# Attention output of the last 64 queries by pairs of heads in the two column halves of the PE array, and their residual added by PE

## The chip, the cores and the metric

One Trainium2 chip, of which one core is used. The metric is the device time of one execution in microseconds (us), here the median of the runs shown. Beside the runs there is one profiled execution, whose trace all durations come from.

## What is computed

Block-wise causal attention on 8 batches with 8 heads, 576 positions and 64 values per head, followed by an MLP-mixer layer. The inputs are float32; the kernel computes in bfloat16 with float32 sums.

```python
scores = q @ k.T / sqrt(64)              # (8, 8, 576, 576)
scores = where(pos_i // 64 >= pos_j // 64, scores, -1e9)
attn   = softmax(scores)
x      = (attn @ v)                      # heads side by side: (8, 576, 512)
h = relu(x.T @ w_tok1) @ w_tok2          # over the 576 positions, 256 hidden
u = x + h.T
out = u + relu(u @ w_ch1) @ w_ch2        # over the 512 channels, 1536 hidden
```

576 is 4.5 times 128. So each batch has four full blocks of 128 query rows and a rest of 64 rows (positions 512 to 575), and the same holds for the keys.

## The kernel before

**How the order is made.** The kernel doesn't issue instructions as it runs through its loops. Every step is added to a planner (class `Plan`) with an engine, an assumed cost, its predecessors, a priority and the PSUM bank that it takes. `Plan.run` plays the steps through in assumed time, `Plan.search` repeats this a thousand times with shaken priorities and keeps the order with the earliest end. The instructions are then emitted in that order, one fixed sequence for each engine. A change of any cost or step therefore gives another order everywhere. A step also has a mode: 0 where the matmul uses the whole 128x128 PE array, 1 for the score matmuls, which use strips of 32 rows, and 2 for matmuls of 64 columns. The planner charges 0.1 us for a change of mode.

**Attention** (`attention`, and `first_attention` for batch 0). A batch's heads are handled as two groups of four (`hg` 0 and 1). For a group, `score_set` (L554) computes transposed scores, keys in the partitions and queries along the free side, with four heads at once in the four 32-row strips of the array; ACT takes the exponentials (L573) into the one buffer `e_sb[hg]`, and DVE clears the masked parts (L579). The keys 512 to 575 are seen only by the last 64 queries; their exponentials for all heads go to `et_sb`.

`head_out` then makes a head's output. The exponentials are the stationary operand (`lhsT`), 128 queries at a time, and the values with a column of ones are the moving operand of 65 columns, so that the last column of the sum is the softmax denominator. Query block I takes key blocks J = 0 to I: 1+2+3+4+5 = 15 matmuls (L602) into one PSUM bank. The fifth block (I = 4) has 64 queries only; the load takes 128 columns all the same, shifted by 64 in odd batches (`shift`), so that the 64 rows lie in partitions 0 to 63 in even and in 64 to 127 in odd batches. The other 64 columns are filler, for which `e_sb` has 64 more columns and `et_sb` is zeroed at the start. DVE takes the reciprocal of the five denominators (L624, 128x5) and multiplies (L630, 128x320) into `x_sb`, whose fifth block is row block 4.

**Token mixing.** `token_up` (L791) multiplies `x_sb` by `w_tok1`: for each half of the hidden side five accumulating matmuls of 512 columns, one for each row block; the fifth uses a copy of the weights with zeros in the half of the partitions that holds filler (`w1_sb[:, 4]` in even batches, `w1o_sb` in odd ones). RELU, then the down product (L884), to which DVE adds `x` (L899). The last 64 rows of two batches share one tile `um_sb` of 128 rows: four pairs. Their down product (L915) already works with the two halves of the PE's columns, one for each batch, and DVE adds the residual by two instructions of 64 partitions (L932).

**Channel mixing.** `channel_up` (L1002), `channel_up_mixed` (L1029), `channel_up_fast` (L1107), `channel_down` (L1322) and `channel_down_fast` (L1231) make the rest. The fast ones use a Strassen-like scheme. The change doesn't touch them.

**The start.** SP loads the keys and queries of batch 0, group 0. All other loads of the start are issued by POOL, one after another: keys and queries (L419), values (L468), weights (L487, L510, L519). Ahead of them POOL makes the identity and zeroes `et_sb` and the ends of `e_sb`; DVE fills the constant parts of `vals` and of `w1_sb` and `w1o_sb` (all at L343). PE runs matmuls on zeros[...] (L372, L379).

Of the kernel before, what the change touches and what calls it, by code (L numbers as in the profile page):

```python
# [22 lines left out]
class Op:  # L23
# [4 lines left out]
        "users", "need", "key", "waiting", "ready", "start", "end", "engine", "n", "mode", "at", "urgent", "until", "quick",  # L28
# [3 lines left out]
class Plan:  # L32
# [13 lines left out]
    def add(  # L46
        self, engines, cost, emit, deps=(), prio=0.0, take=(), give=(), xfer=None, mode=0, at=0.0,
        urgent=0, until=1e9, quick=False,
    ):

        o = Op()
        o.engines = (engines,) if isinstance(engines, str) else tuple(engines)
        o.cost = cost if isinstance(cost, dict) else {e: cost for e in o.engines}
        o.emit, o.prio, o.take, o.give, o.xfer = emit, prio, take, give, xfer
        o.mode, o.at, o.urgent, o.until, o.quick = mode, at, urgent, until, quick
        o.deps = list({id(d): d for d in deps if d is not None}.values())
        o.users, o.n = [], len(self.ops)
        self.ops.append(o)
        return o
# [39 lines left out]
    def run(self):  # L99
# [21 lines left out]
        while left:  # L121
# [13 lines left out]
            for e in ("PE", "ACT", "DVE", "POOL", "SP"):  # L135
                if busy[e] > t or e == "POOL" and landed[-8] > t:
                    continue
                for at, a in enumerate(avail[e]):
                    if self.fits(a[3]):
                        break  # L140
                else:
                    continue
                o = a[3]
# [52 lines left out]
def kernel(  # L196
# [40 lines left out]
    e_sb = ring(2, [128, 4, 1600], BF16, "e_sb")  # L237
# [86 lines left out]
    def reuse(key):  # L324
        return readers.pop(key, [])
# [13 lines left out]
    def init_tiles():  # L339
        def fill(engine, key, prio, *parts):  # L340
            for t, value in parts:
                def emit(o, t=t, value=value):
                    (nc.vector if engine == "DVE" else nc.gpsimd).memset(t, value)  # L343

                pads.setdefault(key, []).append(P.add(engine, 0.17 if engine == "DVE" else 0.5, emit, (), prio))

        for i, t in enumerate(kT):
            fill("DVE", ("kT", i), -1e4 + i, (t[:, S:640, :], 0.0))
        for i in range(2):
            fill(  # L350
                "DVE", ("v", i), -60 + 20 * i,
                (v1[i][64:128, 4, :, :], 0.0),
                (v1[i][:, 0:4, :, 64:65], 1.0),
                (v1[i][0:64, 4, :, 64:65], 1.0),
            )
            fill("POOL", ("e", i), -1e5 + 1, (e_sb[i][:, :, 1536:1600], 0.0))
            fill("POOL", ("et", i), -1e5, (et_sb[i], 0.0))
        fill("DVE", "zeros", -1e5, (zeros, 0.0))
        fill("DVE", "w1", -70, (w1_sb[64:128, 4, :], 0.0), (w1o_sb[0:64, :], 0.0))

        def emit(o):
            make_identity(nc, ident)

        pads["ident"] = [P.add("POOL", 0.6, emit, (), -1e6)]
# [119 lines left out]
    def load_token_weights():  # L484
        def load(dst, src, xfer, prio):
            def emit(o):
                nc.gpsimd.dma_start(out=dst, in_=src)  # L487

            return P.add("POOL", 0.66, emit, (), prio, xfer=xfer)

        done1 = [
            load(w1_sb[:, 0:4, :], moe_w_tok1[0:512, :].rearrange("(c p) t -> p c t", p=128), 32 * 0.06, 5.0),
            load(w1_sb[0:64, 4, :], moe_w_tok1[512:576, :], 4 * 0.06, 5.1),
        ]
        done2 = [
            load(w2_sb, moe_w_tok2.rearrange("(p c) s -> p c s", c=2), 8 * 0.25, 5.2)
        ]
        done1o = [load(w1o_sb[64:128, :], moe_w_tok1[512:576, :], 4 * 0.06, 12.0)]
        return (done1 + pads["w1"], done1 + done1o + pads["w1"]), done2
# [83 lines left out]
    def head_out(b, head, deps, prio, tail, urgent=0):  # L583
        hg, h = divmod(head, 4)

        ei = hg if b == 0 else b % 2
        vt, xt, et, e = v1[b % 2], x_sb[b % 3], et_sb[ei], e_sb[hg]
        ecol = ECOL_LAST if b == 0 and hg == 1 else ECOL
        shift = 0 if b % 2 == 0 else -64
        bank = {}  # L590

        def emit(o, chunks):
            u = bank_of(bank)[:, 0:330].rearrange("p (i c) -> p i c", c=66)
            for I in chunks:
                for J in range(I + 1):
                    if J < 4:
                        c = ecol[J] + 128 * (I - J) + (shift if I == 4 else 0)
                        w = e[:, h, c : c + 128]
                    else:
                        c = 64 + 128 * h + (64 * hg if b else 0) + shift  # L600
                        w = et[:, c : c + 128]
                    nc.tensor.matmul(  # L602
                        out=u[:, I, 0:65],
                        lhsT=w,
                        rhs=vt[:, J, head, 0:65],
                        start=(J == 0),
                        stop=(J == I),
                    )

        steps = ((0, 1, 3), (2, 4)) if b == 0 else (range(5),)  # L610
        av = None
        for chunks in steps:
            av = P.add(
                "PE", 0.0298 * (sum(chunks) + len(chunks)), lambda o, c=chunks: emit(o, c),
                [av, tail] + deps, prio, take=[(BANK, bank)] if av is None else (), urgent=urgent,
            )
        reads(("e", hg), av)
        reads(("et", ei), av)
        reads(("v", b % 2), av)
        ri = rinv[head % 4]  # L620

        def emit_rc(o):
            u = bank_of(bank)[:, 0:330].rearrange("p (i c) -> p i c", c=66)
            nc.vector.reciprocal(ri, u[:, :, 64:65])  # L624

        rc = P.add("DVE", 0.19, emit_rc, [av] + reuse(("rinv", head % 4)), prio - 1, urgent=urgent)

        def emit_mu(o):
            u = bank_of(bank)[:, 0:330].rearrange("p (i c) -> p i c", c=66)
            nc.vector.tensor_tensor(  # L630
                out=xt[:, :, 64 * head : 64 * head + 64],
                in0=u[:, :, 0:64],
                in1=ri.to_broadcast([128, 5, 64]),
                op=MULT,
            )

        mu = P.add("DVE", dve_cost(320), emit_mu, [rc], prio - 1, give=[bank], urgent=urgent)
        reads(("rinv", head % 4), mu)
        return mu

# [6 lines left out]
    def first_tail(hg, heads, deps, prio):  # L647
# [3 lines left out]
        def emit(o):  # L651
# [12 lines left out]
            "PE", 0.1, emit, deps + pads["kT", hg] + pads["et", hg], prio,  # L664
# [12 lines left out]
    def first_attention(ready, v_ready):  # L677
# [3 lines left out]
        for j in range(4):  # L681
# [36 lines left out]
            for h in heads:  # L718
                deps = exps + v_ready[hg] + pad + pads["e", hg]
                done.append(head_out(0, 4 * hg + h, deps, -2900 + j, tails[h], urgent=1))  # L720
        return done

    def attention(b, ready, v_ready):
        et = et_sb[b % 2]
        x_war = reuse(("x", b % 3))
        pad = pads["v", b % 2] + pads["et", b % 2]
# [6 lines left out]
        def tail():  # L733
            deps = ready[0] + ready[1] + pads["et", b % 2] + reuse(("et", b % 2))
# [10 lines left out]
        for hg in range(2):  # L745
# [19 lines left out]
            for h in range(4):  # L765
                deps = exps[h // 2] + v_ready[hg] + x_war + pad + pads["e", hg]
                done.append(head_out(b, 4 * hg + h, deps, prio + 1, tail_done[h // 2]))
# [14 lines left out]
    def token_up(b, cols, tts, xs, war, ready, prio, urgent=0):  # L782
        odd, xt, at = b % 2, x_sb[b % 3], aT[b % 2]
# [3 lines left out]
        def emit(o):  # L787
            for n, tt in enumerate(tts):
                for c in range(5):
                    wt = w1o_sb if c == 4 and odd else w1_sb[:, c]  # L790
                    nc.tensor.matmul(  # L791
                        out=bank_of(bank)[:, w * n : w * n + w],
                        lhsT=wt[:, tt : tt + 255 : 2],
                        rhs=xt[:, c, cols],
                        start=(c == 0),
                        stop=(c == 4),
                    )

        op = P.add("PE", mm_cost(w, 5 * len(tts)), emit, xs + ready[odd] + war, prio, take=[(BANK, bank)], urgent=urgent)
# [11 lines left out]
    def first_uT(x_done, a_done, w2_ready):  # L811
# [3 lines left out]
        for m in range(NDM):  # L815
            bank = {}

            def emit(o, m=m, bank=bank):
# [10 lines left out]
                "PE", mm_cost(128, 4), emit, x_done[2 * m : 2 * m + 2] + pads["ident"], -2700 + m,  # L829
# [27 lines left out]
    def token_mix(b, x_done, w1_ready, w2_ready):  # L857
# [10 lines left out]
        if b == 0:  # L868
            a_all = [
                token_up(0, slice(128 * m, 128 * m + 128), (0, 1), x_done[2 * m : 2 * m + 2], [], w1_ready, -2800 + m, 1)  # L870
# [37 lines left out]
        else:  # L908
# [3 lines left out]
            def emit(o, bank=bank):  # L912
                for t in range(NDT):
                    for i in range(2):
# [5 lines left out]
                            stop=(t == NDT - 1),  # L920
# [3 lines left out]
                "PE", mm_cost(512, 2) + 0.02, emit, a_even[pair] + a_all + w2_ready + um_free[pair], prio + 1.4,  # L924
                take=[(BANK, bank)], mode=2,
            )
            for i in range(2):
                reads(("a", i), op)
                r = slice(64 * i, 64 * i + 64)

                def emit(o, i=i, r=r, bank=bank):
                    nc.vector.tensor_tensor(  # L932
                        out=umt[r, :], in0=bank_of(bank)[r, :], in1=x_sb[(b - 1 + i) % 3][r, 4, :], op=ADD
                    )

                um_rows.append(P.add("DVE", dve_cost(512), emit, [op] + um_rows, prio, give=[bank] if i else ()))
                reads(("x", (b - 1 + i) % 3), um_rows[-1])

# [532 lines left out]
```

## Time and profile before

| | us |
|---|---|
| Median of 5 runs | 293.81 |
| All five | 293.16, 293.62, 293.81, 294.43, 299.16 |
| The profiled execution, its own time | 293.19 |
| Its span in the trace | 291.4 |
| Outside the span (293.19 - 291.4) | 1.8 |
| PE busy in the span | 284.6 |
| DVE busy in the span | 231.8 |
| ACT busy in the span | 170.1 |
| POOL busy in the span | 63.7 |
| Matmuls recorded in the trace | 3224 |

A row of the profile's groups gives the source line, the engine, the operation, what it writes and reads (buffer numbers left out), the array tile for PE, the shapes, how often it occurs, its busy time in us with the mean of one in ns, and the idle time of the engine ahead of it with what ended most of it. "PEld" are the weight loads of PE, which run beside its matmuls. [...]successive ones overlap, so their cost in a dense sequence is the distance of their starts. A few matmul records are missing from the trace. The granted clock of PE was 1.0 throughout.

### The profile page before, as it was taken

The page shows a single profiled execution, that of the slowest core. Times are in us where ns is not written, and L with a number is a line of the kernel's source. Part 1 is how long each engine was busy: PE and PEld are TensorE (multiplying, and loading weights), DVE is VectorE, ACT ScalarE, POOL GpSimd, SP SyncE. Part 2 cuts the span into 40 slices and gives each one's busy share as a digit, 9 for nine tenths or more (in the row PEclk, how much of TensorE's full clock was granted, in tenths as well). Part 3 has the DMA queues.
Part 4 walks back from the last instruction along what each step waited for, and adds up shares of the span by engine and source line. Part 5 has one row for each costly group of instructions (what it writes and reads, how often), then busy time and mean ns, then how long its engine had stood idle before and what let it go on. Part 6 is the DMA issues. An engine that isn't in the chain of part 4 may idle for free.

```text
span 291.4 us, 7678 instructions
## 1 busy us (share of the span) xinstructions
PE 284.6 (98%) x3224; PEld 179.3 (62%) x3244; DVE 231.8 (80%) x505; ACT 170.1 (58%) x241; POOL 63.7 (22%) x100
## 2 busy tenths in 40 slices
PE   8999999999999999999999999999999999999994
PEld 3566446456564766645776466884446888644883
DVE  5566669989687959897997877586989887798994
ACT  5897974758877663677564888432587303377000
POOL 9975545620800150430041000000000000000000
PEclk9999999999999999999999999999999999999999
DMA  8999999995996097991429003041001901230036
GB/s 209 157 201 207 210 186 184 231 188 136 126 172 90 2 128 176 166 177 38 74 20 209 3 2 72 2 164 36 3 0 33 167 2 72 97 122 0 1 100 227
DMA packets 64548, 31.99 MB, mean 110 GB/s; under 512 B 53121, under 2 KB 55297, under 8 KB 64513
## 3 DMA queue, kind: packets, MB, share of 16 engines
q0 software_dynamic: 44320, 17.34, 50.2%
q1 hardware_dynamic: 20192, 14.16, 18.6%
q8 instruction: 25, 0.41, 0.5%
q14 instruction: 11, 0.08, 0.1%
HBM read 35.85 MB, written 9.44 MB: 155 GB/s over the span
## 4 chain that ended last, share of the span: by engine, by line
PE 89%; DMA 5%; POOL 3%; issue 1%; DVE 0%; POOLq 0%
PE mm L1231 19%; PE mm L1002 15%; PE mm L602 9%; PE sc L554 9%; PE mm L1322 7%; PE mm L1107 6%; PE late L1107 6%; PE mm L791 5%; PE late L1231 4%; PE mm L884 4%; PE mm L1029 3%; DMA raws<-in_q_dram 3%; DMA w_sb<-in_moe_w_tok_dram 2%; POOL vals L468 2%; PE mm L915 1%
## 5 line engine op out<-in xcount | busy, mean ns | idle before, releaser
L573 ACT ACTIVATE e_sb<-sc 128x1024 bf16<-128x1024 f32 x95 | 92.4, 1026 | 34.3 <-PE sc L554 33.5
L468 POOL DMA_DIRECT2D vals<-in_v_dram x45 | 37.1, 843 | 41.1 <-PE sc L554 24.8
L1002 PE MATMUL mm<-uT,wc_sb 128*128 128x512 bf16 x192 | 46.1, 382 | 0.0
L439 DVE STREAM_TRANSPOSE turned<-raws 128x288 int32<-128x288 int32 (+1 forms) x65 | 40.4, 698 | 4.4 <-ACT raws L400 1.8
L554 PE MATMUL sc<-turned 32*128 32x64 bf16 (+4 forms) x744 | 35.4, 281 | 0.8 <-ACT e_sb L573 0.5
L602 PEld LDWEIGHTS <-e_sb 128*128 128x128 bf16 x896 | 31.0, 97 | 6.5 <-issue 3.6
L602 PE MATMUL mm<-vals,e_sb 128*128 128x65 bf16 x882 | 32.8, 193 | 0.1
L1002 PEld LDWEIGHTS <-wc_sb 128*128 128x128 bf16 x192 | 20.0, 115 | 20.3 <-issue 5.3
L630 DVE TENSOR_TENSOR x_sb<-mm,rinv 128x320 bf16<-128x320 f32 x63 | 29.7, 483 | 1.4
L1231 PEld LDWEIGHTS <-sums 128*128 128x128 bf16 x252 | 24.0, 98 | 4.9 <-issue 1.4
L1231 PEld LDWEIGHTS <-gT 128*128 128x128 bf16 x240 | 22.8, 98 | 5.0 <-issue 1.4
L777 ACT ACTIVATE gT<-mm 128x512 bf16<-128x512 f32 x36 | 21.6, 599 | 6.3 <-PE mm L1002 4.7
L554 PEld LDWEIGHTS <-turned 32*128 32x128 bf16 x752 | 12.6, 93 | 18.4 <-issue 14.8
L579 DVE MEMSET e_sb<- 64x128 uint32 (+1 forms) x72 | 10.5, 153 | 10.8 <-ACT e_sb L573 7.7
L1254 DVE TENSOR_TENSOR o_sb<-mm,u_sb 128x512 f32<-128x512 f32 x20 | 13.6, 685 | 6.4 <-PE mm L1231 6.3
L791 PE MATMUL mm<-x_sb,w_sb 128*128 128x512 bf16 (+1 forms) x97 | 17.8, 314 | 0.3
L779 DVE TENSOR_SCALAR gT<-mm 128x512 bf16<-128x512 f32 x15 | 10.3, 688 | 9.7 <-PE mm L1002 9.6
L1231 PE MATMUL mm<-wd_sb,sums 128*128 128x256 bf16 x132 | 16.1, 273 | 0.0
L899 DVE TENSOR_TENSOR u_sb<-mm,x_sb 128x512 bf16<-128x512 f32 x24 | 15.4, 681 | 0.8 <-PE mm L884 0.7
L1254 DVE TENSOR_TENSOR o_sb<-mm,o_sb 128x512 f32<-128x512 f32 (+1 forms) x19 | 12.1, 643 | 4.9 <-PE mm L1231 4.8
L1107 PEld LDWEIGHTS <-raws 128*128 128x128 bf16 x96 | 9.3, 98 | 10.4
L777 ACT ACTIVATE gmT<-mm 128x512 bf16<-128x512 f32 x9 | 5.4, 599 | 17.6 <-PE mm L1029 17.6
(145 smaller groups left out, 457.1 us busy)
## 6 DMA issues: line engine op xcount, KB each, us to landing
out_dram<-o_sb SPq DMA_DIRECT2D x14, 512.0 KB, 3.2
raws<-in_k_dram POOLq DMA_DIRECT2D x15, 288.0 KB, 6.7
raws<-in_q_dram POOLq DMA_DIRECT2D x15, 288.0 KB, 7.6
vals<-in_v_dram POOLq DMA_DIRECT2D x28, 128.0 KB, 6.1
wc_sb<-in_moe_w_ch_dram POOLq DMA_DIRECT2D x8, 192.0 KB, 7.1
wc_sb<-in_moe_w_ch_dram POOLq DMA_DIRECT2D x3, 512.0 KB, 10.3
out_dram<-o_sb SPq DMA_DIRECT2D x10, 128.0 KB, 2.4
vals<-in_v_dram POOLq DMA_DIRECT2D x15, 64.0 KB, 4.7
```

Of the source, the lines that this page charges most:

```text
L439: nc.vector.transpose(dst[:, 0:S, :] .rearrange("p s e -> p (s e)") .bitcast(I32) .rearrange("p (a k) -> p k a", k=NB)[:, k0:k1], raw2.bit ...
L468: nc.gpsimd.dma_start(out=dst, in_=src)
L554: nc.tensor.matmul(out=home(n)[:, c0 : c0 + w], lhsT=kT[i][r, j0 : j0 + 128, par], rhs=qT[i][r, i0 : i0 + w, par], start=(par == 0), stop= ...
L573: nc.scalar.activation(dst, sc[SC.index(note["pool"])][:, :, 0:n], EXP, scale=scale)
L602: nc.tensor.matmul(out=u[:, I, 0:65], lhsT=w, rhs=vt[:, J, head, 0:65], start=(J == 0), stop=(J == I),)
L630: nc.vector.tensor_tensor(out=xt[:, :, 64 * head : 64 * head + 64], in0=u[:, :, 0:64], in1=ri.to_broadcast([128, 5, 64]), op=MULT,)
L777: nc.scalar.activation(dst, src, RELU)
L791: nc.tensor.matmul(out=bank_of(bank)[:, w * n : w * n + w], lhsT=wt[:, tt : tt + 255 : 2], rhs=xt[:, c, cols], start=(c == 0), stop=(c == 4),)
L1002: nc.tensor.matmul(out=bank_of(bank), lhsT=wc1_sb[:, m, channels(cc)], rhs=uT[b % 2][:, :, m, :], start=(m == 0), stop=(m == NDM - 1),)
L1107: nc.tensor.matmul(out=bank_of(bank), lhsT=x(m), rhs=y[:, :, m, :], start=first and m == 0, stop=m == 1, skip_group_check=not first,)
L1231: nc.tensor.matmul(out=bank_of(bank)[:, 256 * i : 256 * i + 256], lhsT=x[:, kk, 128 * i : 128 * i + 128], rhs=y[:, kk], start=first and i ...
L1254: nc.vector.tensor_tensor(out=dst, in0=src, in1=other, op=ADD)
```

## The change

- `head_out` computes the four full query blocks only: 10 matmuls per head in place of 15; its reciprocal has 4 columns and its multiply 256.
- A new step `ends_out` makes the last 64 queries. Two heads run side by side: head 2p in array columns 0 to 63 (PSUM partitions 0 to 63), head 2p+1 in columns 64 to 127. A group of four heads is one step of 20 matmuls with loads of 64 columns, in mode 2; in batch 0 it is two steps of 10. A reciprocal (128x2) and a multiply (128x128) follow.
- So row block 4 of `x_sb` has another layout: even heads in partitions 0 to 63, odd heads in 64 to 127, 256 columns in use, in every batch. `token_up` handles it with two matmuls of 256 columns in place of one of 512: with the weights for the lower and for the upper partitions, each into its own 64-column pieces of the output. All batches now wait for both copies of the weights, so that the load of `w1o_sb` is asked for earlier (5.1 in place of 12.0).
- The residual of the paired last rows is added by PE: after the four matmuls of the down product, four more of 256 columns with halves of the identity as stationary operand. One copy, on DVE or ACT, replaces DVE's two adds.
- The planner gets a flag `stick`: such a step is taken only when the last PE step was in a tiled mode, and then ahead of all others; without it in the list PE goes on as before. All `ends_out` steps have it but those of batch 0 and the last one of all.
- Filler goes: `e_sb` has 1536 columns per head, `et_sb` and `e_sb` are not zeroed. The constant fills of `vals`, `w1_sb` and `w1o_sb` move from DVE to POOL, ahead of POOL's loads: 8 memsets in place of 4.

The planner orders everything anew, and the built orders of all engines differ from the start on.

```diff
@@ Plan.run
-                for at, a in enumerate(avail[e]):
+                at = None
+                tiled = e == "PE" and mode > 0
+                for n, a in enumerate(avail[e]):
+                    if a[3].stick > tiled or at is not None and not a[3].stick:
+                        continue
                     if self.fits(a[3]):
-                        break
-                else:
+                        at = n
+                        if a[3].stick or not tiled:
+                            break
+                if at is None:
                     continue
@@ init_tiles
-                pads.setdefault(key, []).append(P.add(engine, 0.17 if engine == "DVE" else 0.5, emit, (), prio))
+                pads.setdefault(key, []).append(P.add(engine, 0.17 if engine == "DVE" else 0.25, emit, (), prio))
...
-                "DVE", ("v", i), -60 + 20 * i,
+                "POOL", ("v", i), -1e5 + i,
...
-            fill("POOL", ("e", i), -1e5 + 1, (e_sb[i][:, :, 1536:1600], 0.0))
-            fill("POOL", ("et", i), -1e5, (et_sb[i], 0.0))
-        fill("DVE", "w1", -70, (w1_sb[64:128, 4, :], 0.0), (w1o_sb[0:64, :], 0.0))
+        fill("POOL", "w1", -1e5 + 2, (w1_sb[64:128, 4, :], 0.0), (w1o_sb[0:64, :], 0.0))
@@ load_token_weights
-        done1o = [load(w1o_sb[64:128, :], moe_w_tok1[512:576, :], 4 * 0.06, 12.0)]
-        return (done1 + pads["w1"], done1 + done1o + pads["w1"]), done2
+        done1o = [load(w1o_sb[64:128, :], moe_w_tok1[512:576, :], 4 * 0.06, 5.1)]
+        return done1 + done1o + pads["w1"], done2
@@ head_out
-        steps = ((0, 1, 3), (2, 4)) if b == 0 else (range(5),)
+        for chunks in ((0, 1), (2, 3)) if b == 0 else (range(4),):
...
-            nc.vector.reciprocal(ri, u[:, :, 64:65])
+            nc.vector.reciprocal(ri[:, 0:4], u[:, :, 64:65])
...
-                in1=ri.to_broadcast([128, 5, 64]),
+                in1=ri[:, 0:4].to_broadcast([128, 4, 64]),
@@ new
+    def ends_out(b, hg, pairs, deps, prio, urgent=0):
...
+        def emit(o):
+            for g, pair in enumerate(pairs):
+                for J in range(5):
+                    for i in range(2):
+                        h = 2 * pair + i
+                        if J < 4:
+                            c = ecol[J] + 128 * (4 - J)
+                            w = e[:, h, c : c + 64]
+                        else:
+                            c = 64 + 128 * h + (64 * hg if b else 0)
+                            w = et[:, c : c + 64]
+                        nc.tensor.matmul(
+                            out=bank_of(bank)[64 * i : 64 * i + 64, 66 * g : 66 * g + 65],
+                            lhsT=w,
+                            rhs=vt[:, J, 4 * hg + h, 0:65],
+                            start=(J == 0),
+                            stop=(J == 4),
+                        )
+
+        av = P.add(
+            "PE", 0.03 * 5 * n, emit, deps, prio, take=[(BANK, bank)], mode=2, urgent=urgent, stick=b > 0 and (b, hg) != (B - 1, 1),
+        )
...
+            nc.vector.reciprocal(ri, view(64, 65))
...
+            nc.vector.tensor_tensor(
+                out=xt[:, 4, c : c + 64 * n].rearrange("p (g d) -> p g d", d=64),
+                in0=view(0, 64),
+                in1=ri.to_broadcast([128, n, 64]),
+                op=MULT,
+            )
@@ token_up
-                for c in range(5):
-                    wt = w1o_sb if c == 4 and odd else w1_sb[:, c]
+                for c in range(4):
                     nc.tensor.matmul(
+                        out=ps, lhsT=w1_sb[:, c, tt : tt + 255 : 2], rhs=xt[:, c, cols], start=(c == 0), stop=False
+                    )
+                for i, wt in enumerate((w1_sb[:, 4], w1o_sb)):
+                    nc.tensor.matmul(
+                        out=ps.rearrange("p (g i d) -> p g i d", i=2, d=64)[:, :, i],
                         lhsT=wt[:, tt : tt + 255 : 2],
-                        rhs=xt[:, c, cols],
+                        rhs=xt[:, 4, cols.start // 2 : cols.stop // 2].rearrange("p (g d) -> p g d", d=64),
@@ token_mix
+                for n in range(2):
+                    for i in range(2):
+                        nc.tensor.matmul(
+                            out=bank_of(bank)[64 * i : 64 * i + 64, :].rearrange(
+                                "p (g n d) -> p g n d", n=2, d=64
+                            )[:, :, n],
+                            lhsT=ident[:, 64 * n : 64 * n + 64],
+                            rhs=x_sb[(b - 1 + i) % 3][:, 4, 0:256].rearrange("p (g d) -> p g d", d=64),
...
-                    nc.vector.tensor_tensor(
-                        out=umt[r, :], in0=bank_of(bank)[r, :], in1=x_sb[(b - 1 + i) % 3][r, 4, :], op=ADD
-                    )
...
+            def emit(o, bank=bank):
+                cast(o, umt, bank_of(bank))
+
+            um_rows.append(P.add(EVAC, evac_cost(512), emit, [op], prio, give=[bank]))
```

## The prediction

> **What bounds the kernel now.** I read the page's engine totals and the chain of work first.
>
> ```profile
> PE 284.6 (98%) x3224; PEld 179.3 (62%) x3244; DVE 231.8 (80%) x505; ACT 170.1 (58%) x241; POOL 63.7 (22%) x100
> ...
> PE   8999999999999999999999999999999999999994
> ...
> PE 89%; DMA 5%; POOL 3%; issue 1%; DVE 0%; POOLq 0%
> ```
>
> PE is busy in every slice and makes nine tenths of the chain. A busy PE need not be a dense PE, so next the chain in order of time (start, duration, what), and the timeline where the tile of the array changes.
>
> ```profile
> 49.19 0.90 PE mm L602 x30
> ```
> ```profile
> 60.34 1.03 PE L1322 MATMUL mm<-wc_sb,gT 128*128 128x512 bf16 x4
> 61.30 0.62 PE L915 MATMUL mm<-aT,w_sb 128*64 128x512 bf16 x4
> 61.85 0.63 PE L554 MATMUL sc<-turned 32*128 32x512 bf16 x8
> 62.42 0.35 PE L602 MATMUL mm<-vals,e_sb 128*128 128x65 bf16 x6
> ```
>
> Thirty matmuls of 65 columns take 0.90 us, 30 ns each. Four of 512 begin at 60.34 and should end their 4 x 0.216 us at 61.20; the next mode begins at 61.30, so the change costs 0.10 us. L915's four run as two concurrent pairs: 0.55 us to the next start, of which 2 x 0.216 are two steps and 0.12 the next change.
>
> I then added up the built order from the first L1002 to the last matmul (26.82 to 287.32 us in the trace, 260.5 us). Concurrent tiles counted once[...], its matmuls take 247.8 us; it has 103 changes of mode, after each of which the trace shows 0.10 us and another 0.01 to 0.03 us at the second step, 0.123 us in the mean, 12.7 us in all. The sum is 260.4 us: from 27 us on PE never waits for anyone. Its waits in the whole trace agree:
>
> ```profile
> PE mm L372 <- DVE wd_sb L343: 1.2, 1, 1.2
> PE sc L554 <- ACT e_sb L573: 0.5, 1, 0.5
> ```
>
> So a PE nanosecond saved after 27 us is a nanosecond of the end, and work of other engines there is free unless it makes PE wait. Before 27 us the bound is a chain over POOL, DMA, DVE and ACT.
>
> [...]
>
> ```profile
> L915 PEld LDWEIGHTS <-w_sb x16: 106/108/110, 61.3 to 205.1; 128*64 128x64 bf16 x16
> ```
> ```profile
> 61.30 0.14 PEld L915 LDWEIGHTS <-w_sb 128*64 128x64 bf16 x4 [0.42 <-issue]
> ```
>
> A load of 64 columns lasts 108 ns against 97 for L602's 128. But all four fit in 0.14 us, so the last starts 0.03 us after the first: the two tiles load together and a tile's second load follows some 28 ns after its first.
>
> **The change, part by part, after the first L1002** (14 of the 16 groups; batch 0 lies before).
> - L602 goes from 840 to 560 matmuls: 280 x 29.6 = -8.28 us.
> - `ends_out`: 280 matmuls as 140 concurrent steps. No row shows narrow matmuls in this mode. Below, a step can't beat its 65 columns, 29.6 ns. Above, if the two loads went one after another, it is [...]57 ns (estimate from the 28 ns between a tile's loads). The nearest row, 64 columns in four strips, has steps of 29 to 33 ns. I take 32: +4.48 us (4.14 to 8.0).
> - `token_up`: in 14 sums one matmul of 512 becomes two of 256, 218 against 216 ns: +0.04 us.
> - The residual: 16 matmuls, 8 concurrent steps of 256 columns at 109 ns: +0.87 us, in L915's mode, so without a change of its own.
> - Modes: the order has 116 changes in place of 103. Of the 13 places where `ends_out` now stands (one holds two groups) 11 follow a score set and lead back to the full array, so that one change becomes two. 13 x 0.115 us (the mean into steps of 65 columns is 0.112): +1.50 us. From below 13 x 0.10, from above 13 x 0.136.
> - DVE per group: 4 x (186 + 483) = 2.68 us becomes 4 x (186 + 417) + about 180 + 283 = 2.88 (417 is the row of a 256-column sum, 283 goes on in its line with 685 for 512): +2.8 us over 14 groups. The residual takes 2 x 0.685 from DVE and gives one copy to DVE or ACT: -2.7 us or more for four pairs. Nothing for the end: DVE stays near 80% and PE has other batches' channel products to run meanwhile. Without that cover it would be 0.2 us a group.
> - The banks and `e_sb`: one more short bank use per group. `e_sb[hg]` is held until the last 64 queries are done, and the next score set of that group, its exponentials and POOL's next loads of values queue behind. The old order ran without a stall at the same pressure; I put 0.1 us.
>
> Sum: -8.28 + 4.48 + 0.04 + 0.87 + 1.50 + 0.10 = -1.29 us.
>
> **The start.** L554 of batch 1 at 26.25 and L1002 behind it wait for two things at nearly the same time.
>
> ```profile
> 1.25 1.19 POOL L343 MEMSET vals<- 128x640 bf16 x2
> 2.39 0.56 POOL L343 MEMSET e_sb<- 128x256 bf16 x2
> 2.90 0.69 POOL L419 DMA_DIRECT2D raws<-in_k_dram  x1
> ```
> ```profile
> 22.91 0.49 DVE L630 TENSOR_TENSOR x_sb<-mm,rinv 128x320 bf16<-128x320 f32 x1
> ...
> 24.94 1.26 DVE L439 STREAM_TRANSPOSE turned<-raws 128x288 int32<-128x288 int32 x2 [0.38 <-DMA raws<-in_q_dram]
> ```
>
> First, the queries of batch 1 land at 24.92. POOL's memsets grow: 640 elements took 625 ns and 256 took 305, so 528, 32, 8 (twice) and 256 (twice) make 2.1 us, and most now wait for the one before (0.07 us, as the identity's second step did): 2.3 us against 1.65, and every load that POOL issues starts 0.65 us later. But the DMA engines are nine tenths busy from 2 us on, first with SP's loads until about 6 us, while POOL's first bytes move at 5.3; so most of it is absorbed in that backlog. `w1o_sb` now stands ahead of these queries: 32 KB at some 190 GB/s, 0.17 us. I take +0.3 us, bounds +0.1 and +0.85. Second, the last multiplies of batch 0, where DVE runs without a break: a pair of heads took 1.34 us, now 2 x (186 + 417) + 150 + 216 = 1.57 us; two pairs give +0.46 us ahead of the transposes. PE's saving there (0.3 us a group) is hidden behind ACT's exponentials, 1.03 us each. DVE's idle 0.38 us takes in part of both: together +0.4 us (0.1 to 1.2).
>
> Total -1.29 + 0.40 = -0.9 us: the profiled time goes from 293.19 to 292.3. The median shown lies 0.62 us above the profiled time; applied to it, 293.81 - 0.9 = **292.9 us**.
>
> **Rivals.**
> - *As forecast* (own range 292.2 to 293.6). Chance 0.46.
> - *Narrow steps at their floor and the start absorbed*: 140 x 29.6, changes at 0.10, start +0.1: -8.28 + 4.14 + 0.91 + 1.3 + 0.1 = -1.8 us, 292.0. For it: the fitted sum of before. Chance 0.11.
> - *The start takes it back*: +1.2 us in place of 0.4 gives -0.1 us, 293.7. For it: POOL heads the chain that ended last; against it, the saturated DMA. Chance 0.20.
> - *Slower by a new wait*: `stick` holds a group's last queries until a score set comes by, `token_up` needs all of `x`, and PE[...] stops. It decides from 0.9/14 = 0.065 us per group; at 0.15 us a group it is +2.1, in all +1.2 us, 295.0. Against it: the planner spread the work to no stall before. Chance 0.13.
> - *Slower, the pairs don't overlap*: the two column tiles load in turn, 57 ns a step, +3.5 us, in all +2.6, 296.4 us. Break-even at 38 ns. Against it: L915's loads 0.03 us apart. Chance 0.10. Here the change wouldn't do what it says.
>
> **Numbers.** About 0.3% (0.9 us) is what a measurement of this kernel can tell from no change. The forecast sits on that bound: of its 0.46 I count 0.33 as faster and 0.13 within; with the second case 0.44 faster; with the third 0.33 within; the two slower cases 0.23. The range, 291.8 to 295.0, reaches from the second case to the fourth and leaves out the fifth.
>
> **What would show it.** L655: twenty matmuls in 0.32 us, after a score set, with 0.1 us on each side (right), or 0.57 us (fifth case). L599 at 30 ns. PE's waits after 27 us: none of size, else the fourth case. The first L1075 at 27.2 us in place of 26.82; at 28 the third case. DVE near 232 us busy. I would be wrong if PE's dense stretch got longer than 259.2 us.

## The result and the profile after

| | before | after |
|---|---|---|
| Median | 293.78 us (79 runs) | 297.15 us (44 runs) |
| Lowest to highest | 293.02 to 299.97 us | 293.09 to 299.83 us |
| Profiled execution | 293.19 us, span 291.4 | 298.39 us, span 296.6 |
| Granted clock in it | 1.000 | 0.977 |
| First channel-up matmul (L1002, L1075) | 26.82 us | 33.19 us |
| From there to the last matmul | 260.50 us | 259.49 us |
| Ratio | | 1.0042, interval 1.0025 to 1.0059 |

The change made the kernel slower; the forecast was 292.9 us. The ratio leaves out executions more than 1.5% above the fastest of their own kernel, which drops 20 of the changed kernel's 44, so it lies below the ratio of the medians, 297.15 / 293.78 = 1.0115.

The page of after, engine totals, PE's slices and PE's granted clock in 40 slices of 7.4 us:

```profile
PE 288.5 (97%) x3267; PEld 182.5 (62%) x3286; DVE 227.9 (77%) x524; ACT 171.6 (58%) x246; POOL 64.2 (22%) x104
...
PE   8799999999999999999999999999999999999995
...
PEclk9955999999999999999999999999999999999999
```

PE has more matmuls and more busy time than before (288.5 against 284.6 us), which looks as if the change had cost PE time. The last line says otherwise: in the third and fourth slices PE ran at about half its clock. The table by stage separates the two. Its columns are the stretch, its length, the busy time of each engine with its count, PE's clock, DMA share and GB/s.

```profile
15.00:28.50 13.50, 13.38 (x164) 8.79 (x165) 5.78 (x33) 7.27 (x12) 9.34 (x17) 0.50 1.27 189
28.50:33.20 4.70, 4.65 (x76) 3.32 (x75) 3.27 (x9) 2.99 (x6) 2.30 (x3) 1.00 1.10 213
33.20:292.70 259.50, 258.25 (x2926) 164.17 (x2940) 212.38 (x466) 151.02 (x211) 40.05 (x56) 1.00 0.63 98
```

All of the loss lies before 33.2 us. From there on PE is busy 258.25 of 259.50 us at full clock, and the stretch is 1.01 us shorter than before. PE's waits in the whole trace:

```profile
PE sc L558 <- DVE turned L443: 1.9, 2, 1.7
PE mm L376 <- DVE wd_sb L349: 1.2, 1, 1.2
PE mm L1395 <- issue: 0.2, 1, 0.2
```

The first line is new: a wait of 1.7 us for transposed keys and queries. The timeline shows where it comes from (start, duration, what, in brackets the idle time ahead and its releaser). First POOL:

```profile
1.37 1.77 POOL L349 MEMSET vals<- 64x528 bf16 x6
3.20 0.31 POOL L349 MEMSET w_sb<- 64x256 bf16 x1
3.56 0.30 POOL L349 MEMSET w1o_sb<- 64x256 bf16 x1
3.81 0.69 POOL L423 DMA_DIRECT2D raws<-in_k_dram  x1
```

The eight memsets last from 1.37 to 3.81 us, so POOL's first load goes out at 3.81 instead of 2.90. Then DVE and PE:

```profile
10.45 1.26 DVE L443 STREAM_TRANSPOSE turned<-raws 128x288 int32<-128x288 int32 x2 [2.72 <-DMA raws<-in_k_dram]
...
13.81 1.26 DVE L443 STREAM_TRANSPOSE turned<-raws 128x288 int32<-128x288 int32 x2 [1.70 <-DMA raws<-in_q_dram]
...
15.12 1.03 PE L558 MATMUL sc<-turned 32*128 32x320 bf16 x8 [1.71 <-DVE turned L443]
```

The keys of batch 0's second group land at 10.42 us (before: 7.78), the queries at 13.78 (before: 12.21), and PE stands from 13.4 to 15.1 us. The granted clock falls at 14.77 us and stays at half for 13.65 us. It is exactly 0.50 here, and the spells of half clock in these runs, 10.24 and 13.65 us, are 3 and 4 times 3.41 us; the full clock ahead of this fall, from 4.53 us on, lasts 10.24 us too. PE was idle for 1.36 us of the 3.41 us ahead of the fall.

The clock also explains most of the spread of the times. In 16 of the 44 executions of after the mean clock is 0.994 or more: median 294.15 us, span 291.8. In the other 28 it is 0.983 or less: median 298.27 us, span 296.15. At full clock the first L1075 would therefore begin near 291.8 - (296.6 - 33.19) = 28.4 us, and the half clock adds another 4.1 us in two executions of three. Of 35 executions of before, measured together with the next four kernels, 5 had a clock below 0.99. The other 30 have a median span of 291.9 us, half a us more than the profiled one, so by the same working before's first L1002 typically begins near 291.9 - (291.4 - 26.82) = 27.3 us. By this estimate the changed kernel starts 1.1 us late at full clock, about as much as the dense stretch gains: its span of 291.8 us is no longer than before's. What makes it slower is mostly the half clock. (The times tell less here than the spans: about half of the 44 executions took 2.0 to 3.6 us outside the span, against 1.8 in before, and no run shows why.)

So the theory to test: *the step of 64 queries does what was forecast; the loss is the place of the memsets, which delays POOL's first loads, makes PE wait at 13 us, and that wait halves the clock.* Rivals: the new steps themselves cost (the narrow pairs, or the forced order of `stick`), or the new order of batch 0 is slow in itself.

### The profile page after: what moved, and what is told of

Read it like the earlier page. It is cut to its first block, busy times and chain, and to the rows that moved or that the text cites. A ratio compares the mean times of both kernels' runs of the same rounds, so it can differ in the third digit from the quotient of the medians.

```text
span 296.6 us, 7792 instructions
## 1 busy us (share of the span) xinstructions
PE 288.5 (97%) x3267; PEld 182.5 (62%) x3286; DVE 227.9 (77%) x524; ACT 171.6 (58%) x246; POOL 64.2 (22%) x104
## 4 chain that ended last, share of the span: by engine, by line
PE 92%; POOL 2%; DMA 2%; DVE 1%; issue 1%; ACT 0%; POOLq 0%; DVEq 0%
PE mm L1304 19%; PE mm L1075 15%; PE sc L558 10%; PE mm L599 7%; PE mm L1395 7%; PE late L1180 6%; PE mm L1180 6%; PE mm L852 5%; PE mm L949 4%; PE mm L1102 3%; PE late L1304 3%; PE mm L655 2%; DMA raws<-in_q_dram 2%; POOL vals L472 1%; PE mm L856 1%
## 5 line engine op out<-in xcount | busy, mean ns | idle before, releaser
L1075 PE MATMUL mm<-uT,wc_sb 128*128 128x512 bf16 x192 | 45.9, 381 | 0.0
L558 PE MATMUL sc<-turned 32*128 32x64 bf16 (+4 forms) x744 | 38.0, 289 | 2.0 <-DVE turned L443 1.9
L1075 PEld LDWEIGHTS <-wc_sb 128*128 128x128 bf16 x192 | 20.1, 115 | 18.9 <-issue 3.9
L599 PEld LDWEIGHTS <-e_sb 128*128 128x128 bf16 x640 | 24.4, 100 | 7.1 <-issue 3.2
L599 PE MATMUL mm<-vals,e_sb 128*128 128x65 bf16 x610 | 26.9, 198 | 0.0
L625 DVE TENSOR_TENSOR x_sb<-mm,rinv 128x256 bf16<-128x256 f32 x61 | 25.4, 420 | 1.4
L558 PEld LDWEIGHTS <-turned 32*128 32x128 bf16 x752 | 13.2, 94 | 18.7 <-issue 13.4
L404 ACT COPY e_sb<-mm 128x512 f32<-128x512 f32 x11 | 6.5, 589 | 27.0 <-PE mm L1180 25.8
L1327 DVE TENSOR_TENSOR o_sb<-mm,u_sb 128x512 f32<-128x512 f32 x24 | 16.2, 686 | 5.2 <-PE mm L1304 5.0
L619 DVE RECIPROCAL rinv<-mm 128x4 f32<-128x4 f32 x61 | 10.7, 177 | 9.7 <-PE mm L599 8.4
L1304 PE MATMUL mm<-wd_sb,sums 128*128 128x256 bf16 x150 | 17.7, 273 | 0.0
L852 PE MATMUL mm<-x_sb,w_sb 128*128 128x512 bf16 (+1 forms) x78 | 16.6, 332 | 0.3
L1327 DVE TENSOR_TENSOR o_sb<-mm,o_sb 128x512 f32<-128x512 f32 (+1 forms) x20 | 12.9, 644 | 4.6 <-PE mm L1304 4.5
```

Source lines behind the costliest of these rows:

```text
L558: nc.tensor.matmul(out=home(n)[:, c0 : c0 + w], lhsT=kT[i][r, j0 : j0 + 128, par], rhs=qT[i][r, i0 : i0 + w, par], start=(par == 0), stop= ...
L599: nc.tensor.matmul(out=u[:, I, 0:65], lhsT=e[:, h, c : c + 128], rhs=vt[:, J, head, 0:65], start=(J == 0), stop=(J == I),)
L625: nc.vector.tensor_tensor(out=xt[:, 0:4, 64 * head : 64 * head + 64], in0=u[:, :, 0:64], in1=ri[:, 0:4].to_broadcast([128, 4, 64]), op=MULT,)
L852: nc.tensor.matmul(out=ps, lhsT=w1_sb[:, c, tt : tt + 255 : 2], rhs=xt[:, c, cols], start=(c == 0), stop=False)
L1075: nc.tensor.matmul(out=bank_of(bank), lhsT=wc1_sb[:, m, channels(cc)], rhs=uT[b % 2][:, :, m, :], start=(m == 0), stop=(m == NDM - 1),)
L1304: nc.tensor.matmul(out=bank_of(bank)[:, 256 * i : 256 * i + 256], lhsT=x[:, kk, 128 * i : 128 * i + 128], rhs=y[:, kk], start=first and i ...
```

## Experiments

### The kernel before with the fills exchanged

The kernel before, its own order of all engines kept; the memsets change places, so that POOL writes the constants of `vals`, `w1_sb`, `w1o_sb` (eight in place of four) and DVE the zeros of `et_sb` and `e_sb` (four in place of eight).

```diff
...
-                    (nc.vector if engine == "DVE" else nc.gpsimd).memset(t, value)
+                    if key[0] in ("e", "et"):
+                        for t2, value2 in first[key]:
+                            nc.gpsimd.memset(t2, value2)
+                    elif key == "w1" or key[0] == "v":
+                        if second:
+                            t2, value2 = second.pop(0)
+                            nc.vector.memset(t2, value2)
...
```

Expected: 

> The kernel before with the fills of vals, w1_sb and w1o_sb on POOL ahead of its loads and those of et_sb and e_sb on DVE, all else in the same order: only the place of the fills is the changed kernel's. Theory 1: POOL's first load goes from 2.9 to 3.8 us, the keys of the second group land 2 to 3 us later, PE waits between 13 and 16 us, and the kernel before becomes slower by 1 us at full clock and by 3 to 5 us where the clock falls: ratio 1.003 to 1.017. Theory 2: 1.000, clock 1.0.

Measured: 294.99 us (13 runs; before 293.87 in 35), ratio 1.0037 (1.0015 to 1.006), as large as the change's 1.0042. The profiled execution took 298.80 us. Three views of it, in this order: the page's line of PE's clock, POOL's first load in the timeline, and PE's longest wait:

```profile
PEclk9966999999999999999999999999999999999999
```
```profile
3.82 0.69 POOL L434 DMA_DIRECT2D raws<-in_k_dram  x1
```
```profile
PE sc L569 <- DVE turned L454: 1.7, 2, 1.2
```

The first load at 3.82 us, the wait for the transposes and the half clock are all there, without any of the rest of the change; the dense stretch is the 260.50 us of before. So the place of the fills alone makes such a loss. The clock was below 0.99 in 4 of 13 executions; the other nine have a median span of 292.7 us, 0.8 over before's 291.9, which is the late load by itself.

### The changed kernel with PE kept busy at 13 us

Eight matmuls of 512 columns on zeros, into a PSUM bank that is overwritten later, ahead of the score set that waits.

```diff
...
+            for _ in range(busy):
+                nc.tensor.matmul(out=home(0), lhsT=zeros[:, 0:128], rhs=zeros, start=True, stop=True)
...
```

Expected: 

> The changed kernel with eight matmuls on zeros (512 columns, 1.73 us) on PE just ahead of the first score set of the second group in batch 0, where PE waited 1.7 us. Theory 1, with the clock as its second part: the wait for the keys and queries stays (first L1075 at 28.4 us), but PE is busy through it, the clock stays at 1.0 in nearly all executions and the time is 0.999 to 1.002 of the kernel before. If the fall of the clock has nothing to do with PE's idle stretch: a mean clock of 0.977 or 0.983 in more than half of the executions, as in the changed kernel, and 1.004 or more.

Measured: 294.32 us (22 runs), ratio 1.0023 (1.0013 to 1.0033); the clock is below 0.99 in none of 22. The page's line of PE's clock; from PE's timeline, the dummy work and the one longer wait; and from DVE's the transposes of the queries:

```profile
PEclk9999999999999999999999999999999999999999
```
```profile
13.42 1.89 PE L554 MATMUL sc<-wd_sb 128*128 128x512 bf16 x7
...
29.29 0.64 PE L560 MATMUL sc<-turned 32*128 32x320 bf16 x16 [1.59 <-DVE turned L443]
```
```profile
12.58 1.26 DVE L443 STREAM_TRANSPOSE turned<-raws 128x288 int32<-128x288 int32 x2 [0.67 <-DMA raws<-in_q_dram]
```

PE's work grew, and the kernel became faster by 2.6 us in the median than the changed kernel on the same chip (next run). With this work in the gap no execution lost the clock, against 6 of 7 without it: the idle stretch at 13 us is what drops it. The median is left 0.45 us above before. The profiled execution, the slowest of the 22, limits the finding. Its queries landed early and their transposes ended at 13.84 us, while the eight matmuls ran to 15.2, so here they held PE up more than they filled a wait, and the first L1075 began at 29.86 us, not at the expected 28.4. And PE waited 1.59 us at 27.7 us with the clock at full: the length of a wait alone doesn't decide.

### The changed kernel again, on the same chip

Expected: 

> The changed kernel as it is, on the same chip as the others. Both theories: about 1.004 of the kernel before; where the clock is 1.0 the first L1075 begins near 28.4 us (259.5 us of dense PE work and 3.9 us of tail from a span of 291.8), where it falls to half for a while near 33 us.

Measured: 296.95 us (7 runs), ratio 1.0088 (1.0056 to 1.012), clock below 0.99 in 6 of 7; in its profiled execution PE's wait was only 0.9 us, the half clock lasted from 17.3 us for 10.24 us, and the dense stretch was 259.52 us. So the loss shows on this chip too, and its size moves with how often the clock falls.

### All fills on DVE: the first load too early

The changed kernel with no fill on POOL.

```diff
-                    (nc.vector if engine == "DVE" else nc.gpsimd).memset(t, value)
+                    nc.vector.memset(t, value)
```

Expected: 

> The changed kernel with its eight constant fills emitted on DVE in place of POOL; the orders of PE, ACT and SP and of all other DVE and POOL work are the same. Theory 1 (POOL's late loads): POOL's first load is issued near 1.3 us in place of 3.8, the keys of the second group land before 8 us in place of 10.4, PE's wait of 1.7 us for the transposes near 15 us is gone, the clock stays at 1.0, the first L1075 begins at 27.0 us or earlier, and the time is about 292.0 us, 0.994 of the kernel before (0.992 to 0.997). Theory 2 (batch 0's own new steps on PE and DVE hold the start back): the first L1075 stays at 28 us or later at full clock, the time within 0.3% of the kernel before or above, and the clock still falls in part of the executions.

Measured: 297.1 us (7 runs), ratio 1.0091 (1.0074 to 1.0108): slower, a miss. POOL's first load now goes out at 1.44 us. The transfers up to 12 us (KB each, median us from issue to landing), first of this kernel, then of the kernel before:

```profile
gT<-in_q_dram SPq DMA_DIRECT2D x1, 288.0 KB, 7.4
gT<-in_q_dram SPq DMA_DIRECT2D x1, 160.0 KB, 7.7
```
```profile
gT<-in_q_dram SPq DMA_DIRECT2D x1, 288.0 KB, 4.0
gT<-in_q_dram SPq DMA_DIRECT2D x1, 160.0 KB, 3.9
```

With POOL's transfers issued early, SP's queries, on which the very first group depends, take 3.4 and 3.8 us longer to land. ACT waits 4.1 us for them (its timeline) and PE 3.9 us (PE's waits):

```profile
9.07 0.67 ACT L404 CAST raws<-gT 128x576 bf16<-128x576 f32 x1 [4.09 <-DMA gT<-in_q_dram]
```
```profile
PE sc L558 <- DVE turned L443: 3.9, 1, 3.9
```

The clock is below 0.99 in 3 of 7 executions, and in the profiled one (304.51 us) it is at half for 23.9 us, 7 times 3.41; the other four have a median span of 294.65 us, 2.8 over before's, so the early load costs time at full clock too. How POOL's transfers hold up SP's isn't shown; the price is those 3.4 us of landing time or more. So some delay ahead of POOL's first load helps: the old memsets were also a pause.

### The kernel before with its first load early

A control: the same line in the kernel before, so that its first load also goes out at 1.44 us.

Expected: 

> The kernel before with the four memsets of POOL moved to DVE, so that POOL's first load is issued at 1.4 us in place of 2.9; nothing else moves. Theory 1b: SP's last query loads of batch 0 land at 9 us or later in place of 6.7, the first exponential begins 3 us later, the clock falls in part of the executions, and the kernel before becomes slower by 0.8% or more. Theory 3: an earlier first load helps or does nothing, 0.997 to 1.000.

Measured: 298.3 us (6 runs; before 293.74 in 43), ratio 1.0135 (1.0092 to 1.0179), the clock below 0.99 in 3 of 6. ACT waits 3.73 us for the same queries, PE 3.4 us; the first L1002 starts at 30.77 us and the dense stretch is 260.51 us. The early load hurts the kernel before as well, where there is no step of 64 queries.

### All fills on DVE, and the old pause on POOL

The changed kernel with the fills on DVE and four dummy memsets on POOL of the sizes that POOL had before, into tiles that are written later.

```diff
+        pace = et_sb + [sums[i][:, 0] for i in range(2)]
...
-                    (nc.vector if engine == "DVE" else nc.gpsimd).memset(t, value)
+                    nc.vector.memset(t, value)
+                    if pace:
+                        nc.gpsimd.memset(pace.pop(0), 0.0)
```

Expected: 

> The changed kernel with its eight fills on DVE, and on POOL four memsets that cost what the kernel before had there (two of 640 elements on et_sb, two of 256 on another unused tile), so that POOL's first load is issued near 2.9 us as in the kernel before; all else in the changed kernel's order. Theory 1b (the moment of POOL's first load decides: at 1.4 us it takes the DMA engines from SP's loads of the first queries, at 3.8 us the second group's keys and queries come late): keys of the second group land near 8 us, PE's longest wait for transposes is under 0.5 us, clock 1.0 in most executions, first L1075 at 26.8 to 27.5 us, 292.0 to 292.8 us, 0.994 to 0.997 of the kernel before. Theory 3 (the changed order of POOL's loads, with the weights ahead of the values, or batch 0's own new steps hold the start back): a wait over 0.8 us or a first L1075 after 28 us remains, and 1.000 or more.

Measured: 293.16 us (22 runs; before 293.74 in 43), ratio 0.9981 (0.9965 to 0.9997); the clock is below 0.99 in 2 of 22, as rarely as in before (4 of 43). The profiled execution takes 293.25 us at clock 1.0. Its POOL timeline, and PE's longest wait:

```profile
2.39 0.56 POOL L353 MEMSET sums<- 128x256 bf16 x2
2.90 0.69 POOL L427 DMA_DIRECT2D raws<-in_k_dram  x1
```
```profile
PE sc L562 <- DVE turned L447: 1.6, 2, 0.8
```

With the first load at 2.90 us again the changed kernel is faster than before, by 0.2% with an interval that ends just below 1. Against the change as made this undoes one thing, the fills' place. Neither forecast came out whole: the time lies between the two, and two waits of 0.8 us are left. It doesn't gain the whole 1.01 us of the dense stretch, since that begins at 28.02 us, 1.2 us later than in before's profile; by the median spans at full clock (291.25 and 291.9 us) it is some 0.45 us (estimate, as above). PE's two waits of 0.8 us lie at 8.3 us, where the clock stayed full, and at 27.4 us, ahead of the stretch. The second comes from the order of POOL's loads: the keys and queries of batch 1 are issued at 17.65 and 19.30 us (before: 15.75 and 16.27), so that DVE waits 0.70 us for them.

### The last 64 queries twice

On top of the paced kernel, `ends_out` runs its twenty matmuls twice into the same sums (numerator and denominator double alike).

```diff
-                for J in range(5):
+                for n_, J in enumerate((0, 1, 2, 3, 4) * 2):
...
-                            start=(J == 0),
-                            stop=(J == 4),
+                            start=(n_ == 0),
+                            stop=(n_ == 9),
```

Expected: 

> As the paced version, with the matmuls of each ends_out done twice over and summed (numerator and denominator both doubled, so their quotient is the same): 140 more concurrent steps after the first L1075, 20 before. If a step costs 31 ns, as the distances of the starts in the changed kernel's trace say, the dense stretch from the first L1075 to the last matmul is 4.3 us longer (263.8 in place of 259.5 us), and so is the time. If the steps' loads had slack beside other work: less than 2 us. If two loads in turn set the pace: 8 us.

Measured: 297.9 us (6 runs), ratio to before 1.0159 (1.0132 to 1.0185), against 0.9981 for the paced kernel. The dense stretch grows from 259.49 to 263.87 us: 4.38 us for 140 more steps, 31.3 ns each. This is the disputed price measured by itself, and it excludes pairs that load in turn, estimated at 57 ns.

### Without `stick`

On top of the paced kernel, the planner is free to put the steps anywhere (`stick=False`), which gives another order.

Expected: 

> As the paced version, with the planner's stick flag off: ends_out is placed by priority alone and the planner makes another order, with 120 changes of mode after the first L1075 in place of 116. From those counts alone 4 x 0.115 us = +0.5 us in the dense stretch; the start may come out otherwise by the new order. Both theories: within 0.4% of the paced version.

Measured: 293.36 us (22 runs), ratio 1.0004 (0.9984 to 1.0024). Its dense stretch is 260.91 us, 1.42 us longer, with 120 changes of mode in place of 115 and new stalls; the longest in the timeline:

```profile
44.29 0.88 PE L603 MATMUL mm<-vals,e_sb 128*128 128x65 bf16 x24 [0.60 <-DMA vals<-in_v_dram]
```

But it begins 1.1 us earlier (26.93 us), since the order of the start changed as well, and the clock is below 0.99 in 5 of 22 executions (paced: 2). So the order that the planner found with `stick` has the better dense stretch and the worse start, and the totals are alike. How much of the 1.42 us is `stick` and how much the luck of the search isn't separated.

### Keys and queries of batch 1 sooner, in both kernels

On top of the paced kernel, POOL issues the first keys and queries of batch 1 ahead of the first channel weights; the same exchange in the kernel before is the control.

```diff
...
-        for op in P.search(1000):
+        order = P.search(1000)
+        for op in sooner:
+            order.remove(op)
+        at = min(order.index(op) for op in later)
+        order[at:at] = sooner
+        for op in order:
...
```

Expected: 

> As the paced version, with one more edit: POOL issues the keys and queries of batch 1, first group, ahead of the first four loads of w_ch1 in place of behind them; every other engine's order is the same. In the paced version's trace these keys landed at 24.7 us and PE waited 0.8 us for their transposes, so the first L1075 began at 28.0 us. Theory 1c (the rest of the loss at the start is these loads coming late): they land before 23 us, PE doesn't wait for the transposes near 27 us, the first L1075 begins at 26.8 to 27.3 us, and the time is 292.0 to 292.5 us, 0.994 to 0.997 of the kernel before. If batch 0's own new steps are what is left: the first L1075 at 27.5 us or later and no difference to the paced version. Against theory 1c would also be a new wait of the first L1075 for w_ch1, which now lands later.

Expected of the control: 

> The kernel before with the same exchange of loads, as a control. There the two chains into the first score set of batch 1 end nearly together (queries at 24.92 us, and PE and ACT with batch 0 at 25.8 to 26.8 us), so the gain should be small: 0.998 to 1.001 of the kernel before. If the exchange itself gained 0.3% here too, the paced version's gain by it would say nothing on the change.

Measured: 292.88 us (17 runs; before 293.63 in 31), ratio 0.9974 (0.9963 to 0.9985), the lowest ratio of all; the control 293.39 us (14 runs), ratio 0.9999 (0.998 to 1.0019). The paced kernel, with this, starts its first channel-up at 27.25 us instead of 28.02. The profiled span is nevertheless 291.5 us for both, since a new wait, here in PE's timeline of the paced kernel with the exchange, gives it back:

```profile
36.51 0.24 PE L567 MATMUL sc<-turned 32*128 32x64 bf16 x8
...
37.27 0.24 PE L567 MATMUL sc<-turned 32*128 32x64 bf16 x8 [0.52 <-DVE turned L451]
```

The 0.77 us gained at the start return as some 0.7 us at 36.6 us, so the dense stretch is 260.34 us instead of 259.49. What the exchange adds in the runs (0.9981 to 0.9974, intervals overlapping) isn't settled.

## Why the prediction was wrong, step by step

- **The dense stretch: right.** Forecast -1.29 us, measured -1.01, in every run that kept the built order (259.48 to 259.52). The prediction's own sign of being wrong, a stretch over 259.2 us, was its forecast without a margin and was passed by 0.3 us. The terms: `ends_out` took 31.3 ns a step where 32 was taken, 4.38 us against 4.48. The trace at 57.82 us shows it: twenty matmuls between a score set and L599, 0.44 us from first start to L599's first.

```profile
57.26 0.64 PE L558 MATMUL sc<-turned 32*128 32x64 bf16 x16
57.82 0.32 PE L655 MATMUL mm<-vals,e_sb 128*64 128x65 bf16 x8
...
58.26 0.47 PE L599 MATMUL mm<-vals,e_sb 128*128 128x65 bf16 x10
```

 The removed matmuls were 30.3 ns apart in the mean (193 ns is what each is recorded with, so they overlap), not 29.6: -8.48 us against -8.28. The changes of mode cost what was taken: 115 in the trace against 102, 13.46 us against 11.92 by the distances of the starts, 0.117 us each in both, so +1.54 us against +1.50 (a matmul of 512 columns whose load is in the trace, but not its own record, counted at 0.216 us). Three short stalls, at 72, 167 and 178 us, make about 0.57 us where 0.10 was taken. With +0.04 and +0.87 as forecast these give -1.09 us; the remaining 0.08 us isn't placed. That the prediction's sum for before closed so well, 260.4 of 260.5 us, was luck in part. Its 247.8 us of matmuls fit the starts of before's trace for 512, 256 and 128 columns, 216, 109 and 56 ns apart in the median; but three matmuls without a record stand in its 0.123 us a change (0.6 us too much), and 0.7 ns are missing from each of 840 matmuls of L602 (0.6 us too little).
- **DVE: harmless, as said.** It is busy 227.9 us (forecast near 232), and PE never waits for it after 33 us.
- **The rival "the pairs don't overlap" (0.10): excluded** by 31.3 ns a step. **The rival "slower by a new wait" (0.13): not this one.** In the built order PE's waits after 33 us come to 0.2 us, so `stick` holds nothing up.
- **The start: the step that failed.** The prediction put: "every load that POOL issues starts 0.65 us later [...] most of it is absorbed in that backlog [...] I take +0.3 us, bounds +0.1 and +0.85", in all +0.4 with the end of batch 0. Three things were wrong in it. The memsets took 2.44 us, not 2.3, and the first load came 0.91 us late. The backlog didn't absorb the delay but enlarged it: 0.91 us at the issue became 2.6 us at the keys' landing and 1.6 us at the queries' (2.2 and 1.6 us where the fills were exchanged in before). These are single profiles: with the first load at 2.90 us the keys landed at 7.78 to 8.87 us in five traces, with 3.8 at 9.19 to 10.42 in four, 1.7 us later in the mean. The saturated DMA was taken for a cover; the later loads took longer instead, from issue to landing 6.6 us for the keys (before: 4.9) and 5.8 us for the queries (5.1). And the wait was sought at batch 1 (24.9 us), whose queries were read as the last to arrive; it came already at batch 0's second group. At full clock the first L1075 then starts about 1.1 us late, not 0.4. Of this the fills make some 0.6 us, since with the old pause 0.45 us are left (estimates from the median spans); the two parts added up, where the prediction let them overlap.
- **What no step priced: the clock.** The profile of before shows a mean clock of 1.0, and the prediction took every PE time at that clock. Where PE's wait at 13 us (1.7 us in the profiled execution) halved the clock, as in 28 of 44 executions, it cost another 4.1 us. The rival "the start takes it back" (0.20) had the right place with +1.2 us, but 293.7 us is short of 297.15 by that clock. The 4.25 us by which the median missed are, roughly, 0.7 us of start, 0.3 us of dense stretch, and for the rest the half clock, with the longer times outside the span.

Left open: what exactly makes the clock fall. A wait of 1.6 us at 27.7 us left it full in one execution, and one of 0.9 us at 14 us was followed by half a clock in another. The runs show that filling the gap at 13 us prevents it, not at what PE load it sets in. The twelve traces narrow it down. Each begins at half clock: in before the first matmuls of 512 columns start 0.43 us apart, and 0.216 us apart once the clock has risen at 5.81 us (so it was 1.0 from there on, not throughout); in the others it rises between 4.05 and 7.06 us. Counted from that rise in stretches of 3.41 us, the step of the spells, each of the five falls stands at the end of a stretch, and in that stretch PE was idle for 0.85, 1.36, 1.36, 2.81 or 3.41 us. No other stretch at full clock has more than 0.92 us; the wait at 27.7 us is split by a boundary, 0.72 and 0.92 us of idle time on its two sides. So it seems to count where in these stretches a wait falls, which differs between executions, and not only how long it is. No run tested this, and a fall at 0.85 us beside none at 0.92 shows that idle time isn't the whole rule. Why the same change of fills costs before less often (4 of 13 executions below 0.99) than the changed kernel (28 of 44) is likewise not separated.

## What to carry to other kernels

Price an edit ahead of the first loads by when the data land, not by when the load is issued: here 0.91 us at the issue became 2.6 us at the landing, and an earlier load (ratios 1.0091 and 1.0135) was no less harmful than a later one (1.0037 and 1.0042). Ask of every new PE wait near the start what it does to the granted clock (below 0.99 in 6 of 7 executions with the wait at 13 us, in none of 22 with it filled), and look at the clock by stage before comparing busy times. A gain in the dense stretch and a loss at the start are told apart by one number, the time of the first matmul of the stretch.

## What the runs showed of the hardware that was not expected

- Of three moments of POOL's first load the middle one was the best in both kernels: 1.44 us (ratios 1.0091 and 1.0135), 2.90 us (before, and 0.9981) and 3.8 us (1.0037 and 1.0042).
- A PE wait of 0.85 us was followed by 10.24 us of half clock, though PE was busy for all of that time (the changed kernel again).
- Eight matmuls on zeros made the changed kernel faster by 2.6 us in the median (296.95 to 294.32), and with them no execution had a half clock.
- In column halves two concurrent matmuls of 65 columns take 31.3 ns with both their loads, though each load is recorded with 106 to 113 ns at full clock.
